# A gated recurrence and a maxout layer: fp32 loads without a cast, gates made with tokens on partitions, u turned by a transposing DMA and v by PE as 4-byte words

## The chip, the cores and the metric

The kernel runs on one core of one Trainium2 chip. The metric is the device time of that core in microseconds (us), lower is better. Engines are named as the profile names them: PE (matmul), PEld (PE's weight loads, which overlap PE), DVE (vector), ACT (scalar, activation functions), POOL (general purpose), SP (which issues DMAs). "q" after an engine's name is its sequencer, where DMAs are issued.

The span of a profile is the profiled execution from first to last instruction.

## The reference

```python
# x, f_logit: (4, 6144, 256) fp32; lower_bound: (256,)
sig = 1.0 / (1.0 + np.exp(-f_logit))
f = lower_bound + (1.0 - lower_bound) * sig
for t in range(S):                       # for each of the 4 sequences and 256 channels
    h = f[:, t] * h + (1.0 - f[:, t]) * x[:, t]
    y[:, t] = h
y = y.reshape(24576, 256)
out = np.maximum(y @ w1, y @ w2) @ w_out # w1, w2: (256, 1024); w_out: (1024, 256)
```

Both kernels use the same algebra. With u = sigmoid(-f_logit) and v = u·x, the recurrence is h = f·h + (1-lb)·v with f = 1 - (1-lb)·u. The factor (1-lb) is moved into the weights. And max(a, b) = a + relu(b - a), so the layer is one matmul by w2-w1, a relu, a projection by w_out, and a linear part y·(w1·w_out), whose small matrix `w13` is computed once at the start.

The scan over time wants channels on partitions and time along the free dimension. The inputs lie in memory with tokens first. Something has to be turned, and that is what the change is about.

## The kernel before

There are 48 blocks of 512 tokens. Each block takes 16 matmuls of 512 columns (hidden), 40 of 256 columns (projection), and 16 transposes of 128x128 on PE, eight for f and eight for x. PE works in the fixed order of the loop at the end; the other engines are scheduled by their dependences.

```python
    def load(c):                                   # DMA casts fp32 to bf16
        # ... (cut)
        for name, src in (("fn", f_logit), ("xn", x)):
            nat = inpool.tile([P, CH // P, D], BF16, name=name)
            nc.gpsimd.dma_start(
                out=nat[:, 0:ni, :],
                in_=src[b, t0 : t0 + nt, :].rearrange("(i p) d -> p i d", p=P),
            )

    def turn(j, slot):                             # two bf16 transposes per slot
        c, o = home[j]
        s, q = divmod(slot, FC // 2)
        if q == 0:
            turned[j, s] = ps_t.tile([P, KC, TB], BF16, name=("fT", "xT")[s])
        dst = turned[j, s]
        for h in range(KC):
            nc.tensor.transpose(
                dst[:, h, q * P : (q + 1) * P],
                ins[c][s][:, o * NSB + q, h * P : (h + 1) * P],
                ident_b[:],
            )

    def recurrence(j):                             # channels on partitions
        fT, xT = turned[j, 0], turned[j, 1]
        # ... (cut)
        nc.scalar.activation(out=u[:], in_=fT[:], func=AF.Sigmoid, scale=-1.0)
        nc.vector.tensor_tensor(out=v[:], in0=u[:], in1=xT[:], op=ALU.mult)
        for h in range(KC):
            nc.vector.tensor_scalar(out=ff[:, h, :], in0=u[:, h, :], scalar1=nom[:, h : h + 1],
                                    scalar2=1.0, op0=ALU.mult, op1=ALU.add)
            nc.vector.tensor_tensor_scan(out=y[:, h, :], data0=ff[:, h, :], data1=v[:, h, :],
                                         initial=..., op0=ALU.mult, op1=ALU.add)

    # ... weight_prep(), hidden(), project() (cut)

    for slot in range(FC):
        turn(0, slot)
    recurrence(0)
    wd, wob, w13 = weight_prep()
    for slot in range(FC):
        turn(1, slot)
    recurrence(1)
    with tc.manual_schedule(engines={ENG.PE}):
        for j in range(NBLK + 1):
            # ... loads of later blocks (cut)
            for fc in range(FC):
                if j < NBLK:
                    hidden(j, fc)          # 2 matmuls of 512 columns, relu on ACT
                if j > 0:
                    project(j - 1, fc)     # 5 matmuls of 256 columns
                if j + 2 < NBLK:
                    turn(j + 2, fc)        # 2 transposes
            if j + 2 < NBLK:
                recurrence(j + 2)
```

## Time and profile before

| | before |
|---|---|
| time | 444.84 us (2 runs, 444.7 to 444.98) |
| span of the profile | 443.3 us |
| PE busy | 95% |
| one block in the middle | 8 x 1.09 = 8.72 us |
| first projection starts at | 27.43 us |
| last block (projection alone) starts at | 434.73 us |

Two lines of the page's parts 1 and 4 say what bounds it: busy time by engine, and the chain of work that ended last, by engine and line (the sum over its PE entries is 94%).

```profile
PE 423.0 (95%) x3488; PEld 309.8 (70%) x3488; DVE 247.0 (56%) x345; ACT 278.5 (63%) x442; POOL 44.9 (10%) x57
...
PE psO L227 47%; PE dT L202 37%; PE xT L103 5%; PE fT L103 5%; DMA wob<-in_moe_w_out_dram 4%; POOL fn L86 1%; POOL xn L86 1%; PE psO L186 0%; DVE osb L237 0%; POOL ident_f masks.py:199 0%; POOL ident_f masks.py:197 0%; POOLq masks.py:199 0%; POOLq L284 0%
```

PE is the bound, and ten points of the chain are the two kinds of transposes. The groups below (line, engine, operation, out<-in, shapes, count | busy us, mean ns | idle before, releaser) show the transposes and the work around them that the change touches.

```profile
L103 PE MATMUL fT<-ident_b,fn 128*128 128x128 bf16 x384 | 52.2, 221 | 13.4 <-DVE ident_b L65 13.4
...
L103 PE MATMUL xT<-ident_b,xn 128*128 128x128 bf16 x384 | 52.2, 221 | 0.0
L113 ACT ACTIVATE u<-fT 128x1024 bf16<-128x1024 bf16 x48 | 49.1, 1024 | 4.9 <-PE fT L103 2.3
...
L115 DVE TENSOR_TENSOR v<-u,xT 128x1024 bf16<-128x1024 bf16 x48 | 32.5, 677 | 3.9 <-PE xT L103 3.9
```

The 221 ns of one transpose is its time from entering PE to leaving it. PE is pipelined, so that is not what it costs. The cost is the distance from one start to the next, and the timeline has it (start us, duration us, engine, line, operation, count). This is PE in the middle of the kernel before:

```profile
220.75 0.28 PE L103 MATMUL fT<-ident_b,fn 128*128 128x128 bf16 x2
220.87 0.59 PE L202 MATMUL dT<-y,wd 128*128 128x512 bf16 x2
221.30 0.38 PE L227 MATMUL psO<-w_182,y 128*128 128x256 bf16 x2
221.52 0.49 PE L227 MATMUL psO<-wob,rt 128*128 128x256 bf16 x3
221.84 0.27 PE L103 MATMUL fT<-ident_b,fn 128*128 128x128 bf16 x2
```

From 220.75 to 221.84 is one slot: 1.09 us, of which the two transposes take 0.11 (220.75 to 220.87), the two 512-column matmuls 0.43, the five of 256 columns 0.54. So 16 transposes cost 0.88 us of a block's 8.72. There is no wait in these lines.

The two queues that carry the loads and the stores (part 3 of the page: packets, MB, share of the 16 engines) have room:

```profile
q0 software_dynamic: 50992, 25.69, 46.1%
q1 hardware_dynamic: 26384, 25.17, 18.4%
```

And this is how PE starts in the kernel before, until its first projection. The bracket at the end of a line is an idle time before it, and what ended it.

```profile
18.02 0.39 PE L202 MATMUL dT<-y,wd 128*128 128x512 bf16 x1 [0.34 <-DVE y L127]
...
20.00 0.59 PE L202 MATMUL dT<-y,wd 128*128 128x512 bf16 x2
...
20.54 0.59 PE L202 MATMUL dT<-y,wd 128*128 128x512 bf16 x2
...
23.51 1.91 PE L186 MATMUL psO<-wob,w1T 128*128 128x256 bf16 x16 [1.83 <-DMA wob<-in_moe_w_out_dram]
...
27.43 0.38 PE L227 MATMUL psO<-w_182,y 128*128 128x256 bf16 x2
```

The linear weights wait 1.83 us for a load, and the first projection starts at 27.43.

### The profile page before, as it was taken

How to read it: one execution, taken by the hardware profiler on the slowest of the kernel's cores; microseconds unless marked ns; L12 is line 12 of the kernel's file. 1: busy time of each engine (PE TensorE's matmuls, PEld its weight loads, DVE VectorE, ACT ScalarE, POOL GpSimd, SP SyncE). 2: the span in 40 equal slices, each digit the busy share in tenths (PEclk: the TensorE clock that was granted, in tenths of full speed). 3: DMA queues.
4: the chain of work that ended last, by engine and by line, in shares of the span. 5: the costliest groups of instructions: out<-in, count | busy, mean ns of one | idle time of the engine just before them, and what ended most of it. 6: DMA issues, size and time to landing. Idle time of an engine off the chain costs nothing.

```text
span 443.3 us, 8434 instructions
## 1 busy us (share of the span) xinstructions
PE 423.0 (95%) x3488; PEld 309.8 (70%) x3488; DVE 247.0 (56%) x345; ACT 278.5 (63%) x442; POOL 44.9 (10%) x57
## 2 busy tenths in 40 slices
PE   0689999999999999999999999999999999999996
PEld 0567777777777777777777777777777777777765
DVE  2744665565556546655655565466546655654631
ACT  3666666666666766666666666666766666666661
POOL 6300101001001001010010010010100100000000
PEclk9999999999999999999999999999999999999999
DMA  8999769487487495694874965956948731212112
GB/s 221 198 198 215 138 124 152 83 146 123 94 140 127 91 163 94 123 151 87 146 119 99 140 121 96 163 95 124 149 85 149 120 95 48 72 49 71 57 64 95
DMA packets 78501, 53.49 MB, mean 121 GB/s; under 512 B 2688, under 2 KB 77440, under 8 KB 78464
## 3 DMA queue, kind: packets, MB, share of 16 engines
q0 software_dynamic: 50992, 25.69, 46.1%
q1 hardware_dynamic: 26384, 25.17, 18.4%
q10 hardware_dynamic: 1088, 2.10, 1.5%
q8 instruction: 27, 0.44, 0.4%
q14 instruction: 10, 0.08, 0.1%
HBM read 53.48 MB, written 25.17 MB: 177 GB/s over the span
## 4 chain that ended last, share of the span: by engine, by line
PE 94%; DMA 4%; POOL 1%; DVE 0%; issue 0%; POOLq 0%
PE psO L227 47%; PE dT L202 37%; PE xT L103 5%; PE fT L103 5%; DMA wob<-in_moe_w_out_dram 4%; POOL fn L86 1%; POOL xn L86 1%; PE psO L186 0%; DVE osb L237 0%; POOL ident_f masks.py:199 0%; POOL ident_f masks.py:197 0%; POOLq masks.py:199 0%; POOLq L284 0%
## 5 line engine op out<-in xcount | busy, mean ns | idle before, releaser
L210 ACT ACTIVATE rt<-dT 128x512 bf16<-128x512 f32 x384 | 226.8, 597 | 142.2 <-PE dT L202 142.1
L227 PE MATMUL psO<-wob,rt 128*128 128x256 bf16 x1536 | 229.8, 273 | 0.0
L202 PE MATMUL dT<-y,wd 128*128 128x512 bf16 x768 | 228.2, 379 | 1.1 <-DVE y L127 1.1
L227 PEld LDWEIGHTS <-rt 128*128 128x128 bf16 x1536 | 150.3, 98 | 57.5
L237 DVE COPY osb<-psO 128x512 f32<-128x512 f32 x96 | 66.4, 692 | 152.5 <-PE psO L227 152.5
L127 DVE TENSOR_TENSOR_SCAN y<-ff,y,v 128x512 bf16<-128x512 bf16 x88 | 108.2, 1272 | 1.5
L227 PE MATMUL psO<-w_182,y 128*128 128x256 bf16 x384 | 73.3, 273 | 0.0
L227 PEld LDWEIGHTS <-y 128*128 128x128 bf16 x384 | 37.6, 98 | 44.4
L103 PE MATMUL fT<-ident_b,fn 128*128 128x128 bf16 x384 | 52.2, 221 | 13.4 <-DVE ident_b L65 13.4
L202 PEld LDWEIGHTS <-wd 128*128 128x128 bf16 x768 | 59.6, 98 | 0.9 <-DVE y L127 0.5
L103 PE MATMUL xT<-ident_b,xn 128*128 128x128 bf16 x384 | 52.2, 221 | 0.0
L113 ACT ACTIVATE u<-fT 128x1024 bf16<-128x1024 bf16 x48 | 49.1, 1024 | 4.9 <-PE fT L103 2.3
L103 PEld LDWEIGHTS <-fn 128*128 128x128 bf16 x384 | 37.3, 99 | 19.2 <-DMA fn<-in_f_logit_dram 11.0
L86 POOL DMA_DIRECT2D fn<-in_f_logit_dram x25 | 21.9, 874 | 237.0 <-PE fT L103 174.2
L119 DVE TENSOR_SCALAR ff<-u,nom 128x512 bf16<-128x512 bf16 x96 | 29.9, 354 | 25.6 <-ACT u L113 25.6
L103 PEld LDWEIGHTS <-xn 128*128 128x128 bf16 x384 | 37.4, 99 | 4.8
L115 DVE TENSOR_TENSOR v<-u,xT 128x1024 bf16<-128x1024 bf16 x48 | 32.5, 677 | 3.9 <-PE xT L103 3.9
L86 POOL DMA_DIRECT2D xn<-in_x_dram x25 | 21.6, 866 | 68.2 <-PE dT L202 64.9
L127 DVE TENSOR_TENSOR_SCAN y<-ff,v 128x512 bf16<-128x512 bf16 x8 | 9.4, 1211 | 0.1
L157 DVE TENSOR_TENSOR wdf<-w2n,w1n 128x1024 f32<-128x1024 f32 x2 | 2.5, 1226 | 6.5 <-DMA w2n<-in_moe_w_dram 6.5
L156 ACT CAST w1b<-w1n 128x1024 bf16<-128x1024 f32 x2 | 2.1, 1045 | 4.6 <-DMA w1n<-in_moe_w_dram 4.6
L186 PE MATMUL psO<-wob,w1T 128*128 128x256 bf16 x16 | 1.9, 272 | 1.8 <-DMA wob<-in_moe_w_out_dram 1.8
(18 smaller groups left out, 15.2 us busy)
## 6 DMA issues: line engine op xcount, KB each, us to landing
out_dram<-osb SPq DMA_DIRECT2D x96, 256.0 KB, 2.7
fn<-in_f_logit_dram POOLq DMA_DIRECT2D x23, 512.0 KB, 8.2
xn<-in_x_dram POOLq DMA_DIRECT2D x23, 512.0 KB, 8.4
w1n<-in_moe_w_dram ACTq DMA_DIRECT2D x2, 512.0 KB, 6.2
w2n<-in_moe_w_dram ACTq DMA_DIRECT2D x2, 512.0 KB, 7.4
fn<-in_f_logit_dram POOLq DMA_DIRECT2D x2, 256.0 KB, 10.3
xn<-in_x_dram POOLq DMA_DIRECT2D x2, 256.0 KB, 10.9
wob<-in_moe_w_out_dram POOLq DMA_DIRECT2D x1, 512.0 KB, 17.0
```

The lines of the kernel that those rows point to most:

```text
L86: nc.gpsimd.dma_start(out=nat[:, 0:ni, :], in_=src[b, t0 : t0 + nt, :].rearrange("(i p) d -> p i d", p=P),)
L103: nc.tensor.transpose(dst[:, h, q * P : (q + 1) * P], ins[c][s][:, o * NSB + q, h * P : (h + 1) * P], ident_b[:],)
L113: nc.scalar.activation(out=u[:], in_=fT[:], func=AF.Sigmoid, scale=-1.0)
L115: nc.vector.tensor_tensor(out=v[:], in0=u[:], in1=xT[:], op=ALU.mult)
L119: nc.vector.tensor_scalar(out=ff[:, h, :], in0=u[:, h, :], scalar1=nom[:, h : h + 1], scalar2=1.0, op0=ALU.mult, op1=ALU.add,)
L127: nc.vector.tensor_tensor_scan(out=y[:, h, :], data0=ff[:, h, :], data1=v[:, h, :], initial=0.0 if prev is None else prev[:, h, TB - 1 : T ...
L156: nc.scalar.copy(out=w1b[:, :, cols], in_=w1n[:, :, cols])
L157: nc.vector.tensor_tensor(out=wdf[:, :, cols], in0=w2n[:, :, cols], in1=w1n[:, :, cols], op=ALU.subtract,)
L202: nc.tensor.matmul(dT[:], lhsT=wd[:, kc, fc * P : (fc + 1) * P], rhs=y[:, kc, :], start=(kc == 0), stop=(kc == KC - 1),)
L210: nc.scalar.activation(out=rt[:], in_=dT[:], func=AF.Relu)
L227: nc.tensor.matmul(ps[:, r, :], lhsT=steps[s][0], rhs=steps[s][1], start=(r == 0 and s == 0), stop=(r == 1 and s == n - 1), skip_group_che ...
L237: nc.vector.tensor_copy(out=osb[:], in_=ps[:])
```

## The change

The intent is to take transposes off PE.

- The sigmoid and the product u·x are made before the turn, with tokens on partitions, in bf16. Then u and v are turned, not f and x.
- From block 3 on, u is turned by a DMA from SBUF to SBUF that transposes. v stays on PE, but its bf16 channels are taken in pairs as 4-byte words: four 128x128 transposes a block where there were eight for the same data.
- The pairs mean that channel d = 2w + h goes to partition w, half h. The weights are loaded in that order.
- The inputs are loaded as fp32 (no cast in the DMA): the first four blocks on the hardware queue of SP, the later ones on the software queue of POOL.
- The projection takes every second token, so that one partition's store is 2 KB in one piece.
- All engines now follow a written order, and the preparation of the weights is rewritten into it.

The diff, cut to its core:

```diff
+    by_dma_u = lambda j: j > 2
+    by_dma_v = lambda j: False
 ...
-            nat = inpool.tile([P, CH // P, D], BF16, name=name)
-            nc.gpsimd.dma_start(out=nat[:, 0:ni, :], in_=...)
+        fn = inpool.tile([P, NQ, D], FP32, name="fn")
+        xn = inpool.tile([P, NQ, D], FP32, name="xn")
+    def load(j, which, eng):
+        eng.dma_start(out=ins[j][which][:],
+            in_=src[b, k * TB : (k + 1) * TB, :].rearrange("(q p) d -> p q d", p=P))
 ...
+    def gate(j):                       # u, tokens on partitions; fp32 read with a step of 2
+            nc.scalar.activation(
+                out=u[:].rearrange("p (h q w) -> p h q w", h=KC, q=NQ),
+                in_=fn[:].rearrange("p q (w h) -> p h q w", h=KC),
+                func=AF.Sigmoid, scale=-1.0)
+    def drive(j):                      # v = u * x, channel pairs side by side
+        nc.vector.tensor_tensor(out=o, in0=u, in1=xi, op=ALU.mult)
+    def turn_pe(j, s, q):              # one transpose of 4-byte words
+        nc.tensor.transpose(
+            turned[j, s][:, q * P : (q + 1) * P],
+            src[:].bitcast(FP32)[:, q * P : (q + 1) * P],
+            ident[:])
+    def turn_dma(j, s):
+        nc.sync.dma_start_transpose(
+            out=t[:].rearrange("p h (q t) -> p (h q) t", q=NQ), in_=(us, vs)[s][j][:])
 ...
-        tok = slice(i * P, (i + 1) * P)
+        tok = slice(2 * g * P + r, 2 * (g + 1) * P, 2)
 ...
-    with tc.manual_schedule(engines={ENG.PE}):
+    with tc.manual_schedule():
+        # loads of blocks 0 to 3 and of the weights, all on nc.sync (cut)
+        gate(0); drive(0); turn_pe(0, ...); forget(0, h); scan(0, h)
+        for g in range(2):
+            for h in range(KC):
+                scale_w1(g, h)
+                diff(g, h)
+            for h in range(KC):
+                turn_w1(g, h)
+        gate(1); drive(1); turn_pe(1, ...); forget(1, h); scan(1, h)
+        gate(2); drive(2)
         for j in range(NBLK + 1):
+                    load(j + 4, s, nc.gpsimd)
             for fc in range(FC):
                 if j < NBLK:
                     hidden(j, fc)
+                    relu(j, fc)
+                if j + 2 < NBLK and not (by_dma_u, by_dma_v)[fc // 4](j + 2):
+                    turn_pe(j + 2, fc // 4, fc % 4)
+                if j == 1 and fc == 0:
+                    linear_weights()
                 if j > 0:
                     project(j - 1, fc)
-                if j + 2 < NBLK:
-                    turn(j + 2, fc)
+                # scans, gate(j + 3), turn_dma(j + 3, 0), drive(j + 3), stores at fixed slots (cut)
```

## The prediction

> **What bounds it now.** TensorE. The page gives PE 423.0 us busy of 443.3 (95%), and the chain of waits is 94% PE, with ten points on the transposes (xT 5%, fT 5%). DVE is at 56%, ACT at 63%; their long idle times are waits for PE (copy out 152.5 us, relu 142.1 us), so they have slack. The granted clock is full everywhere.
>
> The timeline in the middle repeats every 1.09 us, eight times a block (8.72 us). Start to start, one such slot holds two bf16 transposes (0.11 us, 0.055 each), two 512-column matmuls (0.43) and five 256-column matmuls (0.55). Without transposes a block would take 7.84 us. Sum: the first projection at 27.2, 45 blocks of 8.72, two of 7.84, a last one of 4.3, then a copy and a store: 443. The weight loads hide behind the matmuls.
>
> **Removed.** 16 bf16 transposes a block on PE, 0.88 us, all on the critical path; casting loads.
>
> **Added on PE.** Four 4-byte transposes a block. The Trainium skill, "TensorE: Matmul & The Clock Gate" (Terms; Weight-path perf modes), says that transpose mode makes FP32 four times faster, and that fast weight load is off for FP32. No trace here shows one yet. My estimate is one pass with a slower weight load, partly hidden behind the 0.216 us matmul before it: 0.11 us each (0.055 doubled), 0.44 a block. PE block: 8.28 us, 0.44 saved, times 45 blocks: 20 us. The projection's weights are now read with a step of two tokens; I expect that to stay hidden behind 0.108 us matmuls, with little room.
>
> **Moved, off the path.** ACT: sigmoid reads fp32 from SBUF, still about 1.05 us; block sum about 5.9. DVE: the product now reads fp32 with strides; wdf (two fp32 inputs, 1,024 columns) took 1.23 us, so 0.68 becomes about 1.2, perhaps more with the strides; block sum about 5.8 against 5.1. Both stay under 8.28. Two scans (1.27 each) read v from PSUM, about the same.
>
> **DMA.** Loads write 50 MB instead of 25, stores go in 2 KB pieces, and 45 transposes of 256 KB are new: about 91 MB in 420 us, 217 GB/s. The Trainium skill, "DMA: Bandwidth & Descriptors" (Latency and other measured facts), has 261 GB/s for a transposing DMA: an estimate of 1 us of data each, 3 to 6 us to landing beside the loads. The order leaves about 7 us before DVE wants it, and DVE has 2 us to spare, so I expect no PE wait.
>
> **Start and end.** Every weight preparation moves to a fixed order, and the linear weights leave the first block, so the 1.8 us wait for the output weights goes. I expect the first projection about 3 us earlier; the end is unchanged.
>
> **Prediction: 420 us**, 8 in 10 between 408 and 437. Chances: faster by over 2% 0.82, within 2% 0.12, slower 0.06.
>
> **What would show each step.** PE still about 95% busy and head of the chain of waits; the steady block 8.2 to 8.4 us; 4-byte transposes 0.11 us start to start; projection spacing 0.108 us; transposing DMA landing under 7 us; the scaled u waits little for DMA; hidden matmuls wait for no scan and no relu.
>
> **What would make it wrong.** The 4-byte transpose takes several passes (at 0.22 us each the gain is gone); the strided weight load exceeds 0.108 us and paces 40 matmuls a block; the transposing DMA takes 9 us or more beside the loads, DVE waits in order, and PE waits for y; strided fp32 reads double ACT's or DVE's times and delay relu behind the sigmoid. If both the transpose and its weight load hide fully, 412.

## The result, and the profile after

The changed kernel took 431.0 us (two runs, 430.93 and 431.08), against 444.84: a ratio of 0.969, with a 95% interval of 0.966 to 0.972. It is faster by 3.1%. Ratios here are the mean time of one kernel's runs over that of the other's runs of the same rounds, so they are not quite the ratio of the medians that are quoted. Executions over 1.5% slower than the fastest of the same kernel are left out of the means.

The gain is 14 us where 25 was forecast. The time lies inside the range, but the range is 29 us wide, wider than the forecast gain itself, so that says little.

| | before | after | difference |
|---|---|---|---|
| first projection starts at | 27.43 | 32.98 | +5.55 |
| from there to the start of the last block | 407.30 | 387.32 | -19.98 |
| last block and end | 8.57 | 8.80 | +0.23 |
| span | 443.3 | 429.1 | -14.2 |

The same parts 1 and 4 of the page, now of the changed kernel:

```profile
PE 409.6 (95%) x2924; PEld 297.6 (69%) x2924; DVE 276.1 (64%) x344; ACT 279.3 (65%) x441; POOL 69.2 (16%) x96
...
PE psO L206 49%; PE dT L177 39%; PE vT L128 5%; DMA w1n<-in_moe_w_dram 2%; PE dT L265 1%; ACT w1s L247 1%; PE psO L277 0%; DVE vn L120 0%; DVE y L162 0%; SPq L226 0%; ACT w1T L268 0%; PE uT L128 0%; ACT un L100 0%; SPq L82 0%; DVE osb L217 0%
```

PE is still the bound, and the ten points of transposes have become five. The groups that answer to those of before:

```profile
L206 PEld LDWEIGHTS <-rt 128*128 128x128 bf16 x1536 | 150.3, 98 | 44.6 <-issue 0.6
...
L120 DVE TENSOR_TENSOR vn<-un,xn 128x1024 bf16<-128x1024 bf16 x48 | 63.3, 1319 | 23.1 <-ACT un L93 18.6
...
L128 PE MATMUL vT<-ident,vn 128*128 128x128 f32 x192 | 52.5, 280 | 0.7 <-DVE vn L120 0.7
L93 ACT ACTIVATE un<-fn 128x1024 bf16<-128x1024 f32 x45 | 51.0, 1132 | 0.0
L128 PEld LDWEIGHTS vT<-ident,vn 128*128 128x128 f32 x192 | 27.4, 144 | 23.5 <-DVE vn L120 1.5
...
L149 DVE TENSOR_SCALAR ff<-uTs,nom 128x512 bf16<-128x512 bf16 x90 | 27.6, 349 | 14.7 <-DMA uTs<-un 14.6
```

The product takes 1319 ns where it took 677, the sigmoid 1132 where it took 1024. The projection's weight loads, now with a step of two tokens, take 98 ns as before. The last line is the only steady wait on the transposing DMA: 14.6 us of DVE's idle time, over the whole kernel. The middle of the timeline, PE and its weight loads:

```profile
220.84 0.59 PE L177 MATMUL dT<-y,wd 128*128 128x512 bf16 x2
221.06 0.14 PEld L128 LDWEIGHTS vT<-ident,vn 128*128 128x128 f32 x1
221.27 0.27 PE L128 MATMUL vT<-ident,vn 128*128 128x128 f32 x1
...
221.38 0.38 PE L206 MATMUL psO<-w,y 128*128 128x256 bf16 x2
...
221.93 0.59 PE L177 MATMUL dT<-y,wd 128*128 128x512 bf16 x2
```

A 4-byte transpose takes 0.11 us (221.27 to 221.38), exactly as much as the two bf16 transposes that it stands for. Its own weight load, 0.14 us at 221.06, lies wholly behind the second 512-column matmul. A slot with a transpose takes 1.09 us, as before; a slot without takes 0.98. Half of the slots have none now, so a block takes 8.25 us (220.19 to 228.44).

A stretch in the middle confirms that nothing waits. The row has the stretch in us, its length, busy us of PE, PEld, DVE, ACT and POOL, then the granted clock, the DMA share and GB/s.

```profile
200.00:250.00 50.00, 50.00 (x366) 36.57 (x364) 34.06 (x44) 34.34 (x55) 8.98 (x12) 1.00 0.77 219
```

The software queue moved more bytes in a smaller share (it carries 44 of the 48 blocks here; the first four are on the hardware queue), and the transposes came on the hardware queue:

```profile
q1 hardware_dynamic: 66944, 44.32, 38.8%
q0 software_dynamic: 12672, 46.14, 34.2%
```

The start is where the forecast was missed:

```profile
22.21 1.06 PE L177 MATMUL dT<-y,wd 128*128 128x512 bf16 x2
24.52 0.45 PE L128 MATMUL uT<-ident,un 128*128 128x128 f32 x1 [1.25 <-DVE ff L149]
...
25.83 1.06 PE L177 MATMUL dT<-y,wd 128*128 128x512 bf16 x2
...
26.90 1.06 PE L177 MATMUL dT<-y,wd 128*128 128x512 bf16 x2
...
31.23 1.91 PE L277 MATMUL psO<-wob,w1T 128*128 128x256 bf16 x16
32.98 0.27 PE L206 MATMUL psO<-w,y 128*128 128x256 bf16 x1
```

The wait for the output weights is gone, as forecast: the 16 matmuls of the linear weights start without a bracket. But the first hidden matmul starts 4.19 us later than before (22.21 against 18.02), and the slots that follow come every 1.07 us (25.83 to 26.90) where before they came every 0.54. From 29.6 us on they are back at 0.54. Matmuls that start at half the rate, with the same operands and no wait, look like a PE at half its clock; the Trainium skill, "TensorE: Matmul & The Clock Gate" (Part 1), gives 426.7 ns for 512 columns in the cold state and 215.7 ns in the warm one, reached after about 3.4 us of sustained work. The trace agrees with both durations: one 512-column matmul takes 0.43 us here at first and 0.216 us later. Below, a PE at half its clock is called cold. The page's row of the granted clock doesn't show this first cold spell; it reads full speed in these slices.

What the first hidden matmul stands behind is in the chain of work (start us, duration us, what; these are two of its links):

```profile
3.14 8.79 DMA w1n<-in_moe_w_dram
...
19.95 1.31 DVE vn L120
```

The load of w1 lands at 11.9 us, scalings and transposes of the weights follow until 18.96, then block 1's sigmoid, its product (the second line) and its transposes; only then comes block 0's first hidden matmul.

So three questions were open. Which part of the change makes the gain? Why is the start later, and is that all of the missing 11 us? And what limits the next step, turning v by DMA too?

### The profile page after: what moved, and what is told of

The parts are those of the page before. It is cut to its first block, busy times and chain, and to the rows that moved or that the text cites. A ratio compares the mean times of both kernels' runs of the same rounds, so it can differ in the third digit from the quotient of the medians.

```text
span 429.1 us, 7811 instructions
## 1 busy us (share of the span) xinstructions
PE 409.6 (95%) x2924; PEld 297.6 (69%) x2924; DVE 276.1 (64%) x344; ACT 279.3 (65%) x441; POOL 69.2 (16%) x96
## 3 DMA queue, kind: packets, MB, share of 16 engines
q1 hardware_dynamic: 66944, 44.32, 38.8%
q0 software_dynamic: 12672, 46.14, 34.2%
## 4 chain that ended last, share of the span: by engine, by line
PE 94%; DMA 2%; ACT 1%; DVE 1%; SPq 1%; issue 0%
PE psO L206 49%; PE dT L177 39%; PE vT L128 5%; DMA w1n<-in_moe_w_dram 2%; PE dT L265 1%; ACT w1s L247 1%; PE psO L277 0%; DVE vn L120 0%; DVE y L162 0%; SPq L226 0%; ACT w1T L268 0%; PE uT L128 0%; ACT un L100 0%; SPq L82 0%; DVE osb L217 0%
## 5 line engine op out<-in xcount | busy, mean ns | idle before, releaser
L162 DVE TENSOR_TENSOR_SCAN y<-ff,y,vT 128x512 bf16<-128x512 bf16 x88 | 108.0, 1268 | 55.1 <-PE vT L128 55.1
L177 PEld LDWEIGHTS <-wd 128*128 128x128 bf16 x768 | 75.8, 99 | 9.9 <-issue 0.8
L120 DVE TENSOR_TENSOR vn<-un,xn 128x1024 bf16<-128x1024 bf16 x48 | 63.3, 1319 | 23.1 <-ACT un L93 18.6
L206 PE MATMUL psO<-w,y 128*128 128x256 bf16 x384 | 73.5, 273 | 0.4 <-DVE w L284 0.4
L82 POOL DMA_DIRECT2D fn<-in_f_logit_dram x44 | 33.1, 752 | 243.1 <-ACT un L93 243.1
L128 PE MATMUL vT<-ident,vn 128*128 128x128 f32 x192 | 52.5, 280 | 0.7 <-DVE vn L120 0.7
L93 ACT ACTIVATE un<-fn 128x1024 bf16<-128x1024 f32 x45 | 51.0, 1132 | 0.0
L128 PEld LDWEIGHTS vT<-ident,vn 128*128 128x128 f32 x192 | 27.4, 144 | 23.5 <-DVE vn L120 1.5
L82 POOL DMA_DIRECT2D xn<-in_x_dram x44 | 32.9, 749 | 33.6 <-DVE vn L120 33.6
L149 DVE TENSOR_SCALAR ff<-uTs,nom 128x512 bf16<-128x512 bf16 x90 | 27.6, 349 | 14.7 <-DMA uTs<-un 14.6
## 6 DMA issues: line engine op xcount, KB each, us to landing
fn<-in_f_logit_dram SPq DMA_DIRECT2D x4, 512.0 KB, 10.1
xn<-in_x_dram SPq DMA_DIRECT2D x4, 512.0 KB, 10.1
```

The costliest lines, as they stand in the source:

```text
L82: eng.dma_start(out=ins[j][which][:], in_=src[b, k * TB : (k + 1) * TB, :].rearrange("(q p) d -> p q d", p=P),)
L93: nc.scalar.activation(out=u[:].rearrange("p (h q w) -> p h q w", h=KC, q=NQ), in_=fn[:].rearrange("p q (w h) -> p h q w", h=KC), func=AF. ...
L120: nc.vector.tensor_tensor(out=o, in0=u, in1=xi, op=ALU.mult)
L128: nc.tensor.transpose(turned[j, s][:, q * P : (q + 1) * P], src[:].bitcast(FP32)[:, q * P : (q + 1) * P], ident[:],)
L149: nc.vector.tensor_scalar(out=ffs[j][:, h, :], in0=half(j, 0, h), scalar1=nom[:, h : h + 1], scalar2=1.0, op0=ALU.mult, op1=ALU.add,)
L162: nc.vector.tensor_tensor_scan(out=ys[j][:, h, :], data0=ffs[j][:, h, :], data1=half(j, 1, h), initial=0.0 if prev is None else prev[:, h, ...
```

## The experiments

The first theory was: the steady blocks gave what was forecast, because u left PE, and the whole shortfall is at the start. Its main rival was: the transposing DMAs beside the loads cost something in the steady blocks, or leave too little room to turn v in the same way. Each run was correct.

### a_u_pe: u back on PE

```diff
-    by_dma_u = lambda j: j > 2
+    by_dma_u = lambda j: False
```

> u goes back to PE as 4-byte words, v as in the change; no transposing DMA is left. Theory: the steady block is paced by PE alone, and all of its gain comes from taking u off PE. Then four more 4-byte transposes at 0.109 us return: block 8.25 -> 8.69 us, time 431 -> about 450 us, slower than the kernel before by 1 %, although every other part of the change stays. Rival: the gain comes from the loads without a cast, the larger stores or the packing into 4-byte words. Then most of it stays: under 438 us.

It took 450.03 us (449.91 to 450.4), a ratio of 1.012 (1.010 to 1.013) to the kernel before. Every slot has a 4-byte transpose again and takes 1.085 us; a block takes 8.69. So the rest of the change, without the DMA, is worth 0.03 us a block at most, and its start costs about 5 us (first projection at 32.66, against 27.43). The whole of the gain, 19 us, is u leaving PE. This run also measures the cost of the transposing DMAs: the share of the hardware queue is 21.6% here and 38.8% with them. The difference, 0.388 x 429.1 - 0.216 x 448.1 = 69.7 us of all 16 engines for 45 of them, is 1.55 us each (an estimate from shares; 256 KB in that time is 169 GB/s).

### c_v_bf16: v as eight 2-byte transposes

```diff
-        nc.tensor.transpose(turned[...], src[:].bitcast(FP32)[:, q * P : (q + 1) * P], ident[:])
+        for h in range(KC):
+            nc.tensor.transpose(
+                turned[j, s][:].bitcast(BF16)[:, h * TB + q * P : h * TB + (q + 1) * P],
+                src[:, (h * NQ + q) * P : (h * NQ + q + 1) * P], ident_b[:])
```

> u by DMA as in the change; v turned on PE as eight 2-byte tiles a block in place of four 4-byte tiles. Theory: a 4-byte transpose takes 0.109 us start to start because its 128 columns move at half rate, and its weight load is hidden; two 2-byte ones take 2 x 0.055 us, so packing gains nothing: the same time within 0.5 % (431 us), block 8.25 to 8.28 us. Rival: packing is part of the gain. Then the block grows to 8.4 us or more and the time to 438 us or more.

Its four runs were 436.4, 436.7, 431.46 and 430.7 us. The ratio, 0.975 (0.968 to 0.981), is unclear at 2%. (The product also writes v in another order here, as the 2-byte tiles need it.) But the steady block settles the question that it was made for. In its timeline two 2-byte transposes start at 219.41 and the matmuls after them at 219.53; the slot takes 1.09 us and the block 8.25, as with one 4-byte transpose. The two faster runs equal the changed kernel. Packing pairs into words gains nothing on PE. The profiled run, one of the two slower ones, has an early stall, which the next run shows better.

### d_warm: spare matmuls before block 0

```diff
             for h in range(KC):
                 turn_w1(g, h)
+                warm(3)      # 3 matmuls of 512 columns on a spare tile, result never read
```

> Twelve spare 512-column matmuls are put into PE's gaps before block 0, after each group of weight transposes; everything else as in the change, output unchanged. Theory: block 0 runs with matmuls 0.43 us apart instead of 0.216 until 29.4 us because PE had been too idle for its full clock, and this costs about 3.7 us. Then block 0's slots start at 0.54 us, the first projection moves from 33.0 to 30 us or earlier, and the time to about 428 us. Rival: block 0 is paced by relu, sigmoid and the single buffers; the slots stay about 1.07 us and the time stays 431 us or grows by the spare work.

It took 436.23, 431.42, 434.44 and 434.38 us: no gain, against the expectation. The profile shows that the cause was right, though smaller than the 3.7 us expected, and that something else ate it. The slots of block 0 come 0.54 us apart from 24.37 on, but for two (0.81 and 0.91), and the first projection starts at 30.96, 2.0 us earlier than in the changed kernel. By this one profile the cold clock is worth 2.0 of the 5.55 us. But DVE then waits 10.1 us for the first transposing DMA, which was issued at 27.7 and landed 16.3 us later; in the changed kernel it was issued at 29.6 and took 6.9. In stretches of this run (columns as above, the last two are DMA share and GB/s):

```profile
28.00:32.00 4.00, 3.40 (x27) 2.52 (x26) 2.33 (x4) 2.15 (x5) 1.50 (x2) 1.00 1.07 342
...
36.00:40.00 4.00, 4.00 (x31) 2.94 (x29) 0.00 (x0) 2.53 (x6) 0.75 (x1) 1.00 1.23 71
```

The DMA engines are recorded as full in both rows, yet the rate falls from 342 to 71 GB/s while the first transpose runs beside loads of the software queue. From 28 to 44 us that one transpose of 256 KB is recorded with 32.1% of the engines' time, 5.1 us of all 16. Then PE waits 5.1 us and restarts cold; this time the granted clock shows it (0.50 from 48 to 52 us). The profiled run of c_v_bf16 has the same signature (101 and 59 GB/s, 15.5 us to landing).

### e_warm_late: the same, and the first DMA transpose two blocks later

```diff
-    by_dma_u = lambda j: j > 2
+    by_dma_u = lambda j: j > 4
```

> The twelve spare matmuls again, and u is turned by DMA from block 5 on instead of block 3 (two more blocks with u on PE, 0.9 us). Theory: what took the gain of the spare matmuls was the first transposing DMA, which came 2 us earlier, fell into the backlog of prefetched loads and landed after 16 us instead of 7. Two blocks later that backlog has drained: no stall of PE between 36 and 60 us, all runs within 1 us of each other at 429 to 430.5 us. Rival: the stall belongs to the spare matmuls or to the chip; then 434 to 436 us is seen again.

It took 431.46, 435.83, 430.07 and 429.94 us, a ratio of 0.971 (0.964 to 0.977). The profiled run has no stall, but it lost the warm clock too: with the same twelve spare matmuls its block 0 runs at half rate, and the first projection comes at 32.70.

```profile
24.41 1.06 PE L178 MATMUL dT<-y,wd 128*128 128x512 bf16 x2
```

So the transposes started later and beside another start, and the run can't tell which of the two avoided the stall. One run of four is still 435.8; it was not profiled, so whether it stalled in the same way is not shown. The expectation that all runs lie within 1 us failed.

### b_v_dma: v by DMA too

```diff
-    by_dma_v = lambda j: False
+    by_dma_v = lambda j: j > 2
```

> v is turned by DMA too; PE does no transposes after block 2. Theory 1, PE is the only bound: block 7.82 us, about 412 us. Theory 2, the DMA engines have no room for a second transposing transfer (they are 80 % busy in the steady part, of which I estimate the 45 transposes at 22 %): DVE waits for the turned tiles, PE waits for y, and the time ends at 425 us or more. I lean to theory 2.

Its runs took 476.76 and 479.48 us, a ratio of 1.074 (1.071 to 1.078); two more, 496.15 and 559.05, are left out (all four are slower than the kernel before). So the next step of the same idea is a loss of 7%. Three stretches of this run:

```profile
100.00:150.00 50.00, 39.18 (x240) 24.80 (x238) 26.06 (x35) 24.45 (x39) 7.46 (x10) 0.90 1.13 187
200.00:250.00 50.00, 50.00 (x361) 35.08 (x359) 32.38 (x43) 35.72 (x58) 8.37 (x12) 1.00 1.09 263
250.00:300.00 50.00, 37.73 (x240) 24.19 (x238) 23.27 (x32) 24.15 (x39) 7.39 (x10) 0.90 1.11 177
```

and who waited for what (us in total, times, longest):

```profile
DVE ff L149 <- DMA uTs<-un: 100.3, 32, 10.4
...
DVE y L162 <- DMA vTs<-vn: 70.5, 30, 6.8
```

The bytes that a block needs are the same in all three stretches. The middle one moves 263 GB/s and PE never waits; the others move 187 and 177, PE waits 11 or 12 us of 50, and as it comes back cold (granted clock 0.90) it gets through 240 instructions instead of 361. The engines are recorded as full in each. So the limit is not a fixed number of GB/s that the work exceeds. This run has two modes, and the slow one looks like the stall of d_warm. A theory for it: loads of the software queue and transposing DMAs of the hardware queue, interleaved in the same engines, slow each other. The rival: two transposes a block are simply too many.

### h_sync and k_sync_vdma: the loads on the transposes' queue

These two were made for that question. The loads of later blocks move from the software queue to the hardware queue of SP, so that loads, transposes and stores go through one queue; k_sync_vdma then turns v by DMA as well.

```diff
-                    load(j + 4, s, nc.gpsimd)
+                    load(j + 4, s, nc.sync)
```

and, for k_sync_vdma alone,

```diff
-    by_dma_v = lambda j: False
+    by_dma_v = lambda j: j > 2
```

> The loads of block 4 and later go out on the same hardware queue as the transposing DMA and the stores, instead of the software queue; nothing else changes. Theory 1: PE paces the steady part and the queue does not matter: 430 to 432 us. Theory 2: in one queue the transposing DMA stands behind up to 1 MB of loads and lands after 9 us or more; DVE waits and the time is 436 us or more. Theory 3: it is the mix of the software queue with transposing DMA that slows both; then u lands sooner than 5.4 us and no slow runs of 434 us or more are seen.

h_sync took 430.26 us (429.77 to 430.7), a ratio of 0.967 (0.965 to 0.968). It is no more than 1 us faster than the changed kernel, since PE sets the steady pace in both; the first projection, at 32.22, comes 0.76 us earlier. But the time from issue to landing of the transposing DMA changed. In the changed kernel:

```profile
DMA to landing us min/median/max: 3.1/5.4/8.5
```

and in h_sync:

```profile
DMA to landing us min/median/max: 3.1/3.1/5.1
```

DVE never waits for u there, where it waited 14.6 us. And no run of the four was slow. That this is not the chip's doing is shown for the landing: three kernels of the same round on the same chip, with loads on the software queue, have medians of 5.2 (g_cast), 5.7 (e_warm_late) and 5.7 us (f_start).

> v by DMA too, as in b_v_dma, but with the loads of block 4 and later on the same hardware queue as the transposing DMAs. In h_sync these landed after 3.1 us instead of 5.4. Theory 1: what broke b_v_dma was the mix of software-queue loads with transposing DMAs; without it PE paces blocks of 7.82 us and the time is 411 to 414 us. Theory 2: the DMA engines have no room (loads 3.05, stores 1.6, two transposes 3.1 us, 7.75 of 7.82): DVE still waits for turned tiles and the time is 425 us or more.

k_sync_vdma took 410.1 us (408.62 to 410.75), a ratio of 0.921 (0.919 to 0.923). Its code differs from that of b_v_dma in nothing but the queue of the loads, and it is 68 us faster. The two stretches in which b_v_dma lost most:

```profile
100.00:150.00 50.00, 50.00 (x361) 35.06 (x359) 35.40 (x46) 35.82 (x59) 0.00 (x0) 1.00 1.10 276
...
250.00:300.00 50.00, 50.00 (x360) 34.98 (x358) 35.90 (x46) 35.27 (x58) 0.00 (x0) 1.00 1.09 268
```

PE has no transpose and no wait, a block takes 7.82 us, and the loads, stores and 90 transposes are recorded with 97.7% of the engines' time. The rival is out: two transposes a block fit. What did not fit was two transposes a block beside loads of the other queue. One doubt stays: b_v_dma ran on chip 5 and k_sync_vdma on chip 9, and neither was repeated on the other's. Against the chip as the cause speak the kernel before, which took 445.0 us in both rounds, the landings of h_sync above, and the 21 runs of the five kernels with one queue (three chips), none of which is more than 1 us above its kernel's median. Why the mix is slow these runs don't show. The Trainium skill, "DMA: Bandwidth & Descriptors" (SWDGE vs HWDGE vs iDMA), says that each engine takes turns between the internal queues that the software and the hardware side feed; that fits, but no run here separates it from other differences between the two queues.

### g_cast: the cast back in the loads

```diff
-        fn = inpool.tile([P, NQ, D], FP32, name="fn")
+        fn = inpool.tile([P, NQ, D], BF16, name="fn")     # xn likewise
-        load(0, 0, nc.sync)
+        load(0, 0, nc.gpsimd)                             # every load of x and f likewise
```

> All loads of x and f_logit cast to bf16 again on the software queue, as in the kernel before; the rest as in the change. By the queue shares the casting loads take 4.25 us of all 16 engines a block (46.1 % of 443.3 us over 48 blocks), those without a cast 3.05, stores about 1.6, a transposing DMA about 1.55. Theory: the loads without a cast make the room for the transposing DMA; with the cast the sum is 7.4 us of 8.25 and, as DMA comes in bursts, u lands later, DVE waits for it and the time is 436 us or more. Rival, my prediction's view that loads are off the path: 430 to 433 us.

It took 434.01 us (432.63 to 434.52), a ratio of 0.975 (0.973 to 0.977). That lies between the two expectations, so neither held. The steady block is 8.25 us, and DVE waits for u 8.4 us in all, less than in the changed kernel. The loss of 3 us is at the start: the first projection is at 35.99 and not at 32.98, because the first block of f and x lands later. So the loads without a cast gain nothing in the steady blocks. The 3 us at the start belong to the cast and the queue together, since the loads of the first four blocks also moved from SP's queue to the software queue. The cost of loads to the engines did fall: 47.2% of 431.8 us over 48 blocks is 4.25 us a block with the cast (the kernel before gives the same), and 34.2% of 429.1 over the 44 blocks of the changed kernel's software queue is 3.34 without (estimates from shares), though the latter write twice the bytes. The 3.05 of the expectations divides by 48 and is too low. With 3.34 the sum for two transposes a block is 8.0 us, more than the 7.82 that a block of k_sync_vdma took: a recorded share depends on what else is in flight and is not a fixed price.

### f_start: the start in another order

The weights get one tile per half, so that the first half's scaling doesn't wait for the second half's load; block 0's hidden matmuls come before block 1's transposes; DMA transposes begin with block 5.

```diff
-    w1n = wpool.tile([P, KC, DFF], FP32)
+    w1n = [wpool.tile([P, KC, DFF // 2], FP32, name=f"w1n{g}") for g in range(2)]
 ...
+        weights(0); gate(1); drive(1); weights(1)
+        for fc in range(FC):
+            hidden(0, fc); relu(0, fc)
+            if fc == 3: turn(1); recur(1)
+            if fc > 3: turn_w1(fc // 2 - 2, fc % 2)
+        gate(2); drive(2); turn(2)
```

> Only the start is changed: the weights of each half in tiles of their own (so that the first scaling does not wait for the second half), read in order instead of with a step of four, block 1's inputs ahead of the second half, the 16 weight transposes and the turning of block 1 moved behind the first four hidden matmuls; u by DMA from block 5 on (0.9 us more). Theory: the change's 11 us above my prediction are its start. Then the first hidden matmul comes at 12 to 15 us instead of 22, the first projection at 21 to 26 us instead of 33, and the time is 421 to 425 us with a steady block of 8.25 us. Rival: the start only waits for HBM; then the first projection stays after 30 us and the time at 429 us or more.

It took 430.13 us (429.09 to 431.27), a ratio of 0.966 (0.965 to 0.968). The first hidden matmul starts at 12.31, 10 us earlier than in the changed kernel, and the first projection at 30.28, only 2.7 us earlier: a miss. PE waits 2.33 us for a relu that stands behind the scaling of the second half in ACT's fixed order, and 1.75 us for the third sigmoid, which stands behind the copies of turned weights; and in such gaps its clock falls again. An early first instruction is worth little when the fixed order of another engine holds the next one.

### n_sync_warm and l_sync_start: clock alone, and order with clock, on one queue

n_sync_warm is h_sync with the spare matmuls of d_warm. l_sync_start is h_sync with the order of f_start mended further (four hidden slots of block 0 ahead of the second half's scaling, the turned weights spread between slots, block 2's product later) and eight spare matmuls.

```diff
+        turn(0); recur(0); warm(8)
+        weights(0); gate(1); drive(1)
+        for fc in range(4): hidden(0, fc); relu(0, fc)
+        for h in range(KC): turn_w1(0, h)
+        turn(1); weights(1); recur(1)
+        for fc in range(4, FC): hidden(0, fc); relu(0, fc); ...   # turn_w1(1, h) in between
 ...
+                if j == 1 and fc == 2:
+                    drive(2); turn(2); recur(2); ahead(3)          # sigmoid, turn, product of block 3
```

> h_sync plus the twelve spare matmuls of d_warm, and nothing else. In d_warm block 0 ran at 0.54 us a slot and the first projection came 2.0 us earlier, but a stall between 44 and 53 us took more than that. With the loads on the hardware queue I expect no stall: h_sync's 430.3 us less 2.0, 427.8 to 428.8 us. If the cold clock cost nothing, 430.3 us.

n_sync_warm took 429.69 us (429.22 to 429.98), a ratio of 0.966 (0.964 to 0.967), 0.6 us below h_sync, which ran on another chip; the intervals of the two overlap. The gain of 1.5 to 2.5 us that was expected is not there. Its start on PE:

```profile
21.51 0.59 PE L178 MATMUL dT<-y,wd 128*128 128x512 bf16 x2
23.80 0.30 PE L129 MATMUL uT<-ident,un 128*128 128x128 f32 x1 [1.70 <-DVE ff L150]
23.94 1.01 PE L178 MATMUL dT<-y,wd 128*128 128x512 bf16 x2
...
24.95 1.06 PE L178 MATMUL dT<-y,wd 128*128 128x512 bf16 x2
```

PE is warm at 21.51. One wait of 1.70 us later the slots come at 1.06 us again, until 27.5, and here the granted clock shows it (0.50 from 24 to 26 us). But d_warm had the same waits (1.15 and 1.69 us) and stayed warm, and e_warm_late went cold already before the second of them. So with gaps of this size PE may or may not stay warm, and the gain of spare matmuls ahead of them can't be relied on.

> h_sync with another start: the order of f_start taken further (relu of the first half of block 0 ahead of the second half's scaling, half of the weight transposes there too, block 2 turned inside block 1, so that no matmul of block 1 waits for block 2's loads), and eight spare matmuls after the first turning. Theory: the first projection comes at 25 to 28 us instead of 33 and the time falls by as much, to 422 to 426 us. Rival: the start is bound by the arrival of its 7 MB; then the first projection stays at 30 us and the time at 427 us or more.

l_sync_start took 427.36 us (425.81 to 427.81), a ratio of 0.960 (0.958 to 0.962). The first projection starts at 24.23, 3.2 us before that of the kernel before, better than expected; the time is not. Where it went:

```profile
33.04 0.30 PE L129 MATMUL vT<-ident,vn 128*128 128x128 f32 x1 [3.30 <-DVE vn L121]
...
33.73 0.98 PE L178 MATMUL dT<-y,wd 128*128 128x512 bf16 x2
```

Block 3's product comes too late in DVE's order, PE waits 3.30 us, and its clock falls again for some slots after (the second line's two matmuls span 0.98 us where a warm pair spans 0.59). Of the 8 us by which the first projection came earlier than in h_sync (32.22), 3 are in the time.

### o_sync_start_vdma: the parts that worked, together

This is k_sync_vdma with the start of l_sync_start, where block 3's sigmoid, product and turns go ahead of block 2's scans.

```diff
+                if j == 1 and fc == 0:
+                    gate(3); turn_dma(3, 0)
-                if j == 1 and fc == 2:
-                    drive(2); turn(2); recur(2); ahead(3)
+                if j == 1 and fc == 1:
+                    drive(2); drive(3); turn_dma(3, 1); turn(2); recur(2)
```

> Both findings together: k_sync_vdma with the start of l_sync_start, mended where that lost time (block 3's sigmoid and product ahead of block 2's scans, so that nothing in block 2 waits for them). In l_sync_start the first projection came at 24.2 us instead of 33, but 3.3 us went to one wait in block 2 and some more to the slow clock after it. If that wait is gone, 410.1 us less about 8: 401 to 404 us. If the DMA engines, over 100 % busy by the shares of k_sync_vdma, cannot take the earlier start, 406 us or more.

It took 403.89 us (five runs, 403.09 to 404.62), a ratio of 0.907 (0.906 to 0.909) to the kernel before, as expected. The first projection starts at 24.26, and PE has no long wait in the block after. It beats both kernels. From there to the last block (394.63) a block takes 7.88 us on average, so of the 8.3 us that the first projection came earlier than in k_sync_vdma (32.52) some 2 are lost again. Its hardware queue is recorded with 102.4% of the engines' time, and DVE waits for the transposing DMA 113.9 us in all; little of this reaches PE, which in the stretch from 300 to 350 us was busy 49.18 us of 50. What a further DMA stream would cost no run shows.

## Why the prediction was right, and where a term was off

- **What bounds the kernel: right.** PE is 95% busy in both, with 94% of the chain.
- **The steady blocks: right, and nearly exactly.** 20 us were forecast for them (45 blocks of 0.44), and 19.98 were measured between the first projection and the last block. The block was forecast at 8.28 us and measured at 8.25. That u alone makes the gain is shown by a_u_pe.
- **The 4-byte transpose: right in size.** 0.11 us start to start. The reason given was off. The estimate put it down to a slower weight load, partly hidden. The load is slower (144 ns against 98) but wholly hidden; what doubles is the transpose itself, start to start, and it does so whether a load of 98 ns or one of 144 follows (four in a row take 0.43 us in f_start, from 18.05). The factor of four for FP32 that the prediction quotes is not tested: no run has an FP32 matmul outside transpose mode. The consequence was not drawn: at 0.11 us, one packed transpose costs just what the two that it replaces cost, so v's packing saves nothing, as c_v_bf16 shows.
- **The strided weight load: right.** 98 ns before and after. The Trainium skill, "TensorE: Matmul & The Clock Gate" (Weight-path perf modes), lists packed and strided chunks alike for the fast load, and the trace agrees for a step of two.
- **DVE and ACT off the path: right.** The product takes 1.32 us where "about 1.2, perhaps more with the strides" was forecast, the sigmoid 1.13 where 1.05 was. In the stretch from 200 to 250 us DVE is busy 34.06 us of 50 and ACT 34.34, which is 5.6 and 5.7 us of an 8.25 us block (5.8 and 5.9 were forecast).
- **The transposing DMA: right that PE doesn't wait.** It lands after 5.4 us (3 to 6 were forecast) and DVE waits 14.6 us for it in all. Its engine time was taken too small: about 1.55 us each against the forecast 1 us that was worked out from the skill's 261 GB/s. In this kernel that costs nothing. The risk named, DMA landing late and PE waiting for y, did come true in b_v_dma, d_warm and the profiled run of c_v_bf16, with a cause that the prediction had not seen: the mix with the loads of the software queue. That the changed kernel itself, with the same mix, ran twice without the stall may be luck: of the twelve runs of c_v_bf16, d_warm and e_warm_late, which carry the mix too, six took 434 us or more.
- **The start: mis-sized, and the cause of 8.6 of the missing 11 us.** The prediction put it as "I expect the first projection about 3 us earlier". It came 5.55 us later, so this one term was off by 8.5 us. The forecast span is 443.3 - 19.8 - 3 = 420.5, the measured one 429.1, and the difference is 8.6. The wait for the output weights did go (1.83 us), as the prediction said. What it did not count are two costs. The first hidden matmul starts 4.19 us later: it now stands behind a fixed chain of weight loads, scalings and transposes. And PE, with little to do before, runs block 0 at half its rate. d_warm shows the second by itself: 2.0 us. That order is the rest is shown in part: reordering in f_start, without spare matmuls, brought the first projection 2.7 us forward, and in l_sync_start to 24.23 us, earlier than before the change, but with spare matmuls added too.
- **The remaining 2 us** are that the sum was one of a span, while the time runs 1.7 to 1.9 us above it, and the rounding of 420.5 to 420. The prediction gave it as a time.

What stays open: why loads of the software queue and transposing DMAs of the hardware queue slow each other, and why b_v_dma goes in and out of that mode. In the runs made, one queue for both removes it; that the chip has no part in b_v_dma's collapse is likely, not shown.

## What to carry to other kernels

When an engine is the bound and its slots have no waits, count its work start to start; whatever leaves the engine leaves the time, one for one, and packing that halves the count of instructions gains nothing if each takes twice as long. Cost the start separately, as a chain of loads and fixed orders with a cold PE, because a reordering that is free in the steady state can lose there over a quarter of what the steady state wins (5.55 of 20 us here). Before judging that DMA has no room for another stream, look at whether its rate is steady under a full share; if it isn't, try the streams on one queue.

## What the Trainium skill lacked or had wrong

- "TensorE: Matmul & The Clock Gate" (Part 4) has no cost for transposes start to start, and none for 4-byte ones, and says that the full clock doesn't engage for them. In the kernel before, PE does nothing but bf16 transposes from 13.38 to 17.5 us: the first eight take 0.10 us each, and from 16.62 on sixteen take 0.056 each. So transposes alone brought the full rate. In a busy PE one of 4-byte words takes 0.109 us with its weight load hidden; while PE was cold, about 0.21 us.
- "DMA: Bandwidth & Descriptors" (Latency and other measured facts) has 261 GB/s for a transposing DMA, measured with a non-contiguous middle dimension. The 256 KB here took about 1.55 us of all engines (an estimate from the queue shares: 169 GB/s). "Advanced Engine Details and Errata" (X-Bar Transpose) says that such DMAs are as fast as regular ones; by the same shares the plain fp32 loads of the changed kernel took 3.34 us for 1.05 MB, which is 314 GB/s.
- The rule of "DMA: Bandwidth & Descriptors" (Rules for kernel authors) that a transpose next to ordinary DMAs needs nothing holds for results: all runs were correct. Of speed it says nothing. Beside loads of the software queue the rate fell as low as 59 GB/s (c_v_bf16) and landings grew to 20.9 us (b_v_dma); with the loads on the transposes' own queue the work of b_v_dma ran at 266 to 276 GB/s, 68 us faster in all.
- No page that was used has what a cast in a load costs the engines: 4.25 us a block with the cast against 3.34 without (estimates from shares), though the latter writes twice the bytes.
- "TensorE: Matmul & The Clock Gate" (Part 1) says that a cold spell follows an idle window of about 3.4 us, in a free-running window. No run here tests the window itself, but much shorter waits were enough: in n_sync_warm one of 1.70 us, the second in 3 us, was followed by half rate, while the same waits left d_warm at full rate. The profile's row of the granted clock showed full speed in the first slices of the changed kernel while matmuls ran at half rate, and 0.50 in the later cold spells of n_sync_warm and d_warm: at the start the spacing of the matmuls is the surer sign.
